# v loads on ACT's hardware queue, W_spatial and W_out requested at a later place, and the first q cast on VectorE

## The chip, the cores and the metric

The kernel runs on one core of one Trainium2 chip. The metric is the device time of one launch, in microseconds (us). A time is the median of all runs of a kernel; ratios and their intervals use runs in the fast state alone, and profiled runs are in the fast state unless the text says otherwise. Every kernel here gave a correct result. Times of different chips are not set against each other.

## The reference

Two layers follow one another. The first is a linear attention with decay, in blocks, over 4 batches, 8 heads, 768 tokens and 64 channels. The second is a gated MLP with a product over the tokens (W_spatial) in its middle.

```python
# attention: per block of 64 tokens, with a state carried from block to block
intra = einsum('bhic,bhjc->bhij', qb, kb) * Dmask
out   = einsum('bhij,bhjd->bhid', intra, vb) + einsum('bhid,bhde->bhie', qb * lam_pow, kv_state)
kv_state = lam_block * kv_state + einsum('bhsd,bhse->bhde', kb * rev_pow, vb)
# gated MLP on x = the attention's output, 4 x 768 x 512
h = maximum(x @ w_in, 0);  u, v = split(h)          # 512 columns each
v_n = normalise(v)
out = (u * (einsum('ts,bsd->btd', w_spatial, v_n) + b_spatial)) @ w_out
```

q, k and v are 6.3 MB each and are read once; W_spatial, its bias and W_out are read once for all batches.

## The kernel before

The kernel goes in 12 steps of 256 tokens (4 batches of 3). Each step loads k, q and v, all on SP's queue, in that order; casts them (k times a decay on VectorE or GpSimd, q on ACT, v on GpSimd); transposes k and q on TensorE; and computes scores, state and output. `xT` is the output of a step, brought by ACT from PSUM to SBUF in bf16; the products `pv` and `pu` with the two halves of W_in read it. The products with W_spatial and W_out of a batch are put between the attention steps of the next, and fill TensorE there.

Only TensorE and GpSimd keep the order of the text (`manual_schedule`). The order of instructions on ACT, VectorE and SP is chosen at compile time.

```python
    lam_bc = const.tile([P, H], FP32)
    nc.scalar.dma_start(out=lam_bc, in_=lam.unsqueeze(0).to_broadcast((P, H)))
    def load_step(n):
        # ... tiles q_in, k_in, v_in from a pool of 4 buffers each ...
        for c in range(2):
            nc.sync.dma_start(out=k_in[:, :, c, :], in_=...)      # 256 KB, rows of 256 bytes
        nc.sync.dma_start(out=q_in..., in_=...)                   # 512 KB, rows of 512 bytes
        for c in range(2):
            nc.sync.dma_start(out=v_in[:, :, c, :], in_=...)      # 256 KB, rows of 256 bytes
    load_step(0)
    krev = iota_f(...); qpos = iota_f(...); rel = iota_f(...)     # GpSimd iota, cast on VectorE
    load_win(DH, DFF)                                             # half of W_in, GpSimd's queue
    for n in range(1, 4):
        load_step(n)
    # ... ACT: loglam = Ln(lam_bc), ldec = Exp(loglam * krev), lq from qpos ...
    def cast_step(n):
        eng = nc.vector if n < NR else nc.gpsimd
        eng.tensor_tensor(out=kd..., in0=s["k_in"], in1=ldec..., op=ALU.mult)
        nc.scalar.activation(out=qc..., in_=s["q_in"], func=AF.Copy)
        nc.gpsimd.tensor_copy(out=vc, in_=s["v_in"])
    # trans_step: pt <- kd, qc (TensorE); kT <- pt (ACT); qT <- pt * lq (VectorE)
    # scores_step: pam <- qT, kT (TensorE); a <- pam * mask (VectorE)
    # kv_step: pkv <- vc, kd (TensorE).  out_step: pat <- qT, s, a, vc (TensorE); xT <- pat (ACT)
    with tc.manual_schedule(engines={PE, mybir.EngineType.Pool}):
        cast_step(0)
        load_win(0, DH)
        cast_step(1)
        nc.gpsimd.dma_start(out=wsp_raw, in_=...)                 # W_spatial, 1152 KB
        nc.gpsimd.dma_start(out=bsp_bc, in_=...)
        nc.gpsimd.dma_start(out=wout_sb, in_=...)                 # W_out, 512 KB
        trans_step(0); scores_step(0); kv_step(0); trans_step(1)
        load_step(4)
        for n in range(NS):
            if n + 2 < NS: cast_step(n + 2)
            if n + 5 < NS: load_step(n + 5)
            if n + 1 < NS: scores_step(n + 1)
            out_step(n)
            # ... queue pv, pu and the products with W_spatial and W_out ...
            if n + 1 < NS: kv_step(n + 1)
            fill(f // 2)
            if n + 2 < NS: trans_step(n + 2)
            fill(f - f // 2)
```

Of the kernel before, what the change touches and what calls it, by code (L numbers as in the profile page):

```python
# [9 lines left out]
FP32 = mybir.dt.float32  # L10
BF16 = mybir.dt.bfloat16
I32 = mybir.dt.int32
AF = mybir.ActivationFunctionType
# [5 lines left out]
def kernel(  # L19
# [12 lines left out]
    nc = tc.nc  # L32
    P = 128
    B, H, S, D = q.shape
# [6 lines left out]
    NR = S // (2 * P)  # L41
    NS = B * NR
    T2 = 2 * P
# [4 lines left out]
    fin = ctx.enter_context(tc.tile_pool(name="fin", bufs=4))  # L48
# [14 lines left out]
    st = {}  # L63

    def load_step(n):
        b, r = divmod(n, NR)
        toks = slice(r * T2, (r + 1) * T2)
        q_in = fin.tile([P, H, 2, D], FP32, tag="q_in", name=f"q_in_{n}")
        k_in = fin.tile([P, H, 2, D], FP32, tag="k_in", name=f"k_in_{n}")
        v_in = fin.tile([P, H, 2, D], FP32, tag="v_in", name=f"v_in_{n}")  # L70
        for c in range(2):
            nc.sync.dma_start(out=k_in[:, :, c, :],  # L72
                              in_=k[b, :, toks][:, c * P:(c + 1) * P].rearrange("h p d -> p h d"))
        nc.sync.dma_start(out=q_in.rearrange("p h m d -> p h (m d)"),  # L74
                          in_=q[b, :, toks].rearrange("h (p m) d -> p h (m d)", m=2))
        for c in range(2):
            nc.sync.dma_start(out=v_in[:, :, c, :],  # L77
                              in_=v[b, :, toks][:, c * P:(c + 1) * P].rearrange("h p d -> p h d"))
        st[n] = {"q_in": q_in, "k_in": k_in, "v_in": v_in}

    load_step(0)
    ident = const.tile([P, P], BF16)
    make_identity(nc, ident)

# [14 lines left out]
    wout_sb = wpool.tile([P, NCH, DM], BF16)  # L99
    bsp_bc = wpool.tile([P, S], BF16)  # L100
    wt_sb = wpool.tile([P, NBLK, S], BF16)
    wsp_raw = wpool.tile([P, NBLK, S], BF16)

    def load_win(f0, f1):
        nc.gpsimd.dma_start(out=win_sb[:, :, f0:f1],
                            in_=moe_w_in.rearrange("(g p) f -> p g f", p=P)[:, :, f0:f1])

    load_win(DH, DFF)
    for n in range(1, 4):
        load_step(n)  # L110
# [11 lines left out]
    for g in range(NG):  # L122
        nc.scalar.activation(out=lq[:, g, :], in_=qpos.rearrange("p m a d -> p (m a d)"),
                             func=AF.Exp, scale=logl[:, g:g + 1])
# [19 lines left out]
    def cast_step(n):  # L144
        s = st[n]
        kd = att.tile([P, 2, H, D], BF16, tag="kd", name=f"kd_{n}")
        qc = att.tile([P, 2, H, D], BF16, tag="qc", name=f"qc_{n}")
        vc = att.tile([P, H, 2, D], BF16, tag="vc", name=f"vc_{n}")
        eng = nc.vector if n < NR else nc.gpsimd
        eng.tensor_tensor(out=kd.rearrange("p c h d -> p h c d"), in0=s["k_in"],  # L150
                          in1=ldec.unsqueeze(2).unsqueeze(3).broadcast_to((P, H, 2, D)),
                          op=ALU.mult)
        nc.scalar.activation(out=qc.rearrange("p m h d -> p h m d"), in_=s["q_in"], func=AF.Copy)  # L153
        nc.gpsimd.tensor_copy(out=vc, in_=s["v_in"])  # L154
        s["kd"], s["qc"], s["vc"] = kd, qc, vc

    def trans_step(n):
        kd, qc = st[n]["kd"], st[n]["qc"]
        pt = two_banks([P, 2, NG, T2], f"pt_{n}", BF16)
        for j, src in ((0, kd), (1, qc)):  # L160
            for g in range(NG):
                for c in range(2):
                    nc.tensor.transpose(  # L163
                        out=pt[:, j, g, c * P:(c + 1) * P],
                        in_=src[:, c, 2 * g:2 * g + 2, :].rearrange("p h d -> p (h d)"),
                        identity=ident)
        kT = att.tile([P, NG, T2], BF16, tag="kT", name=f"kT_{n}")
        nc.scalar.activation(out=kT, in_=pt[:, 0], func=AF.Copy)  # L168
        qT = att.tile([P, NG, 2, 2, D], BF16, tag="qT", name=f"qT_{n}")
        nc.vector.tensor_tensor(out=qT.rearrange("p g m a d -> p g (m a d)"), in0=pt[:, 1],  # L170
                                in1=lq, op=ALU.mult)
        st[n]["qT"], st[n]["kT"] = qT, kT
# [4 lines left out]
    def scores_step(n):  # L177


        kT = st[n]["kT"]  # L180
        a_sb = att.tile([P, 2, 2, 2, 2, P], BF16, tag="a_sb", bufs=2, name=f"a_{n}")
        st[n]["a"] = a_sb
        for i in range(2):
            pam = two_banks([P, 2, 2, 2, P], f"pam_{n}_{i}")
            for g2 in range(2):
                for c in range(2):
                    for hh in range(2):
                        g = 2 * i + g2
                        nc.tensor.matmul(out=pam[:, hh, g2, c, :],  # L189
                                         lhsT=kT[hh * D:(hh + 1) * D, g, c * P:(c + 1) * P],  # L190
                                         rhs=qblk(n, g, hh, c), start=True, stop=True)
            nc.vector.tensor_tensor(  # L192
                out=a_sb[:, i].rearrange("p h g c x -> p (h g) c x"),
                in0=pam.rearrange("p h g c x -> p (h g) c x"),
                in1=amask[:, i].rearrange("p h g x -> p (h g) x").unsqueeze(2)
                .broadcast_to((P, 4, 2, P)), op=ALU.mult)
# [144 lines left out]
    def fill(n):  # L341
        for _ in range(min(n, len(pend))):
            pend.pop(0)()
# [12 lines left out]
            pend.extend([lambda i=i: po(b, i) for i in range(NR)])  # L356

    with tc.manual_schedule(engines={PE, mybir.EngineType.Pool}):
        cast_step(0)
        load_win(0, DH)  # L360
        cast_step(1)
        nc.gpsimd.dma_start(out=wsp_raw, in_=moe_w_spatial.rearrange("(a p) s -> p a s", p=P))
        nc.gpsimd.dma_start(out=bsp_bc, in_=moe_b_spatial.unsqueeze(0).to_broadcast((P, S)))
        nc.gpsimd.dma_start(out=wout_sb, in_=moe_w_out.rearrange("(t p) f -> p t f", p=P))
        trans_step(0)
        scores_step(0)
        kv_step(0)
        trans_step(1)
        load_step(4)
        fills = {0: 1, 1: 2, 2: 5}  # L370
        for n in range(NS):
            if n + 2 < NS:
                cast_step(n + 2)
            if n + 5 < NS:
                load_step(n + 5)
            if n + 1 < NS:
                scores_step(n + 1)
            out_step(n)
            after_out(n)
            if n + 1 < NS:  # L380
                kv_step(n + 1)
            f = fills.get(n, 4 + (n % 3 == 0))
            fill(f // 2)
            if n + 2 < NS:
                trans_step(n + 2)
            fill(f - f // 2)
        fill(len(pend))
# [30 lines left out]
```

## Time and profile before

| kernel before | |
|---|---|
| time, median of 3 runs (range) | 184.18 us (183.65 to 187.49) |
| time and span of the profiled run | 188.46 us, 186.7 us |
| TensorE busy | 145.7 us, 78% |
| ACT busy | 89.1 us, 48% |
| first instruction of TensorE | 14.3 us |

The profiled run took 4 us more than the median.

Three more views are needed for the comparison; the third stands behind the prediction. The first is the page's chain of work that ended last, as shares of the span (SPq and ACTq are issues of transfers):

```profile
PE 54%; SPq 13%; DVE 11%; ACT 9%; DMA 9%; issue 2%; POOL 1%; ACTq 0%; POOLq 0%
```

The second is the sum over one early stretch (start and end, length, then busy time and count of PE, PEld, DVE, ACT and POOL, granted clock, DMA share, GB/s). The third is the timeline: start, length, engine and line, operation, out<-in, and in brackets the idle time before it with what ended it. First VectorE's row, then ACT's two.

```profile
13.50:24.40 10.90, 6.39 (x83) 5.61 (x85) 10.04 (x20) 4.22 (x6) 2.17 (x2) 1.00 1.04 215
```

```profile
4.50 0.15 DVE L89 CAST krev<-krev_i 128x1 f32<-128x1 int32 x1
```

```profile
25.96 1.31 ACT L252 ACTIVATE xT<-pat 128x1024 bf16<-128x1024 f32 x1 [3.41 <-PE pat L249]
28.19 1.06 ACT L153 ACTIVATE qc<-q_in 128x1024 bf16<-128x1024 f32 x1 [0.92 <-DMA q_in<-in_q_dram]
```

The small cast `krev`, which the decay `ldec` needs, is done at 4.6 us. ACT brings the first `xT` at 25.96 us, **before** the next cast that has to wait for a q.

### The profile page before, as it was taken

The page shows a single profiled execution, that of the slowest core. Times are in us where ns is not written, and L with a number is a line of the kernel's source. Part 1 is how long each engine was busy: PE and PEld are TensorE (multiplying, and loading weights), DVE is VectorE, ACT ScalarE, POOL GpSimd, SP SyncE. Part 2 cuts the span into 40 slices and gives each one's busy share as a digit, 9 for nine tenths or more (in the row PEclk, how much of TensorE's full clock was granted, in tenths as well). Part 3 has the DMA queues.
Part 4 walks back from the last instruction along what each step waited for, and adds up shares of the span by engine and source line. Part 5 has one row for each costly group of instructions (what it writes and reads, how often), then busy time and mean ns, then how long its engine had stood idle before and what let it go on. Part 6 is the DMA issues. An engine that isn't in the chain of part 4 may idle for free.

```text
span 186.7 us, 3638 instructions
## 1 busy us (share of the span) xinstructions
PE 145.7 (78%) x1540; PEld 96.5 (52%) x1540; DVE 103.4 (55%) x191; ACT 89.1 (48%) x98; POOL 34.8 (19%) x35
## 2 busy tenths in 40 slices
PE   0005677507979779999997999999799999999980
PEld 0005563305649556655776665575676646565430
DVE  1029993705399853542989747169884722564400
ACT  4244324712677942268775613666722157660051
POOL 4004060006245344060606005020000000000000
PEclk9999996975999979999999999999999999999999
DMA  4999969999999999999998900530000027000035
GB/s 98 218 211 252 205 161 184 199 212 232 199 241 248 200 239 238 221 225 222 330 254 195 252 8 0 208 133 4 0 0 4 2 79 262 0 0 4 0 132 205
DMA packets 68337, 28.36 MB, mean 152 GB/s; under 512 B 50528, under 2 KB 65248, under 8 KB 68320
## 3 DMA queue, kind: packets, MB, share of 16 engines
q1 hardware_dynamic: 65664, 25.17, 56.5%
q0 software_dynamic: 2512, 2.95, 9.6%
q8 instruction: 12, 0.20, 0.5%
q14 instruction: 5, 0.04, 0.1%
q10 hardware_dynamic: 144, 0.00, 0.0%
HBM read 24.78 MB, written 6.29 MB: 166 GB/s over the span
## 4 chain that ended last, share of the span: by engine, by line
PE 54%; SPq 13%; DVE 11%; ACT 9%; DMA 9%; issue 2%; POOL 1%; ACTq 0%; POOLq 0%
PE pvs L307 17%; PE po L322 11%; DMA v_in<-in_v_dram 9%; PE pv L277 8%; PE pu L297 7%; SPq L77 6%; SPq L72 5%; PE pt L163 4%; DVE a L192 3%; PE pvs L309 3%; SPq L74 3%; DVE st L282 3%; ACT vh L280 2%; ACT wt_sb L336 2%; DVE vn L288 2%
## 5 line engine op out<-in xcount | busy, mean ns | idle before, releaser
L307 PE MATMUL pvs<-wt_sb,vn 128*128 128x384 bf16 x192 | 37.8, 331 | 2.1 <-ACT wt_sb L336 2.0
L192 DVE TENSOR_TENSOR a<-pam,amask 128x1024 bf16<-128x1024 f32 x24 | 28.5, 1210 | 6.0 <-PE pam L189 6.0
L154 POOL CAST vc<-v_in 128x1024 bf16<-128x1024 f32 x12 | 12.9, 1074 | 84.0 <-DMA v_in<-in_v_dram 42.7
L252 ACT ACTIVATE xT<-pat 128x1024 bf16<-128x1024 f32 x12 | 15.8, 1320 | 23.7 <-PE pat L249 23.6
L307 PEld LDWEIGHTS <-vn 128*128 128x128 bf16 x192 | 18.9, 99 | 14.9 <-issue 2.5
L297 PE MATMUL pu<-xT,win_sb 128*128 128x256 bf16 x192 | 24.4, 285 | 1.9 <-DVE a L192 1.9
L311 DVE TENSOR_TENSOR gT<-pvs,uT 128x768 bf16<-128x768 f32 x16 | 15.3, 958 | 18.2 <-PE pvs L309 18.1
L277 PE MATMUL pv<-win_sb,xT 128*128 128x512 bf16 x96 | 24.2, 400 | 1.2 <-ACT xT L252 1.2
L322 PE MATMUL po<-wout_sb,gT 128*128 128x512 bf16 x96 | 21.9, 379 | 1.5 <-DVE a L192 1.1
L297 PEld LDWEIGHTS <-win_sb 128*128 128x128 bf16 x192 | 19.2, 102 | 5.7 <-issue 1.8
L153 ACT ACTIVATE qc<-q_in 128x1024 bf16<-128x1024 f32 x12 | 12.7, 1055 | 19.0 <-DMA q_in<-in_q_dram 19.0
L325 ACT ACTIVATE o<-po 128x1024 f32<-128x1024 f32 x12 | 12.3, 1025 | 19.0 <-PE po L322 19.0
L282 DVE BATCH_NORM_STATS2 st<-vh 128x6 f32<-128x512 bf16 x24 | 15.6, 682 | 10.4 <-ACT vh L280 10.3
L163 PE MATMUL pt<-ident,kd 128*128 128x128 bf16 x96 | 8.6, 242 | 15.5 <-DVE kd L150 15.5
L170 DVE TENSOR_TENSOR qT<-pt,lq 128x1024 bf16<-128x1024 bf16 x12 | 8.2, 684 | 18.5 <-ACT kT L168 18.5
L150 POOL TENSOR_TENSOR kd<-k_in,ldec 128x1024 bf16<-128x1024 f32 x9 | 17.1, 1897 | 6.1 <-DMA k_in<-in_k_dram 6.1
L168 ACT ACTIVATE kT<-pt 128x1024 bf16<-128x1024 bf16 x12 | 12.2, 1021 | 11.2 <-PE pt L163 11.2
L280 ACT ACTIVATE vh<-pv 128x1024 bf16<-128x1024 f32 x12 | 12.3, 1024 | 8.8 <-PE pv L277 8.8
L163 PEld LDWEIGHTS <-kd 128*128 128x128 bf16 x96 | 7.2, 110 | 17.4 <-DVE kd L150 15.7
L277 PEld LDWEIGHTS <-xT 128*128 128x128 bf16 x96 | 9.5, 102 | 11.7 <-issue 1.7
L322 PEld LDWEIGHTS <-gT 128*128 128x128 bf16 x96 | 9.2, 98 | 11.9 <-issue 1.0
L299 ACT ACTIVATE uT<-pu 128x1024 bf16<-128x1024 f32 x12 | 12.2, 1020 | 5.9 <-PE pu L297 5.8
(52 smaller groups left out, 146.2 us busy)
## 6 DMA issues: line engine op xcount, KB each, us to landing
k_in<-in_k_dram SPq DMA_DIRECT2D x24, 256.0 KB, 5.8
q_in<-in_q_dram SPq DMA_DIRECT2D x12, 512.0 KB, 6.1
v_in<-in_v_dram SPq DMA_DIRECT2D x24, 256.0 KB, 6.0
out_dram<-o SPq DMA_DIRECT2D x12, 512.0 KB, 3.4
wsp_raw<-in_moe_w_spatial_dram POOLq DMA_DIRECT2D x1, 1152.0 KB, 11.3
win_sb<-in_moe_w_in_dram POOLq DMA_DIRECT2D x2, 512.0 KB, 8.4
wout_sb<-in_moe_w_out_dram POOLq DMA_DIRECT2D x1, 512.0 KB, 14.8
bsp_bc<-in_moe_b_spatial_dram POOLq DMA_DIRECT2D x1, 192.0 KB, 11.7
```

Of the source, the lines that this page charges most:

```text
L150: eng.tensor_tensor(out=kd.rearrange("p c h d -> p h c d"), in0=s["k_in"], in1=ldec.unsqueeze(2).unsqueeze(3).broadcast_to((P, H, 2, D)), ...
L154: nc.gpsimd.tensor_copy(out=vc, in_=s["v_in"])
L163: nc.tensor.transpose(out=pt[:, j, g, c * P:(c + 1) * P], in_=src[:, c, 2 * g:2 * g + 2, :].rearrange("p h d -> p (h d)"), identity=ident)
L192: nc.vector.tensor_tensor(out=a_sb[:, i].rearrange("p h g c x -> p (h g) c x"), in0=pam.rearrange("p h g c x -> p (h g) c x"), in1=amask[: ...
L252: nc.scalar.activation(out=xT[b][:, r].rearrange("p g (c d m) -> p (g c) m d", c=2, m=2), in_=po.rearrange("p g c (m d) -> p (g c) m d", m ...
L277: nc.tensor.matmul(out=ps[:, j], lhsT=x[:, r, c, j * P:(j + 1) * P], rhs=win_sb[:, c, DH:DFF], start=(c == 0), stop=(c == NCH - 1))
L280: nc.scalar.activation(out=vh[:, pair, :], in_=ps, func=AF.Relu)
L282: nc.vector.bn_stats(out=m["st6"][:, t, :], in_=vh[:, t, :])
L297: nc.tensor.matmul(out=ps[:, f], lhsT=win_sb[:, c, f * P:(f + 1) * P], rhs=x[:, r, c, :], start=(c == 0), stop=(c == NCH - 1))
L307: nc.tensor.matmul(out=ps[:, i, 0:HW_], lhsT=m["vn"][:, s, f * P:(f + 1) * P], rhs=wt_sb[:, s, cols], start=(s == 0), stop=False)
L311: nc.vector.tensor_tensor(out=m["gT"][:, f, :].rearrange("p (i x) -> p i x", i=2), in0=ps[:, :, 0:HW_], in1=m["uT"][:, f, :].rearrange("p ...
L322: nc.tensor.matmul(out=ps[:, j], lhsT=gT[:, c, t * P:(t + 1) * P], rhs=wout_sb[:, c, :], start=(c == 0), stop=(c == NCH - 1))
```

## The change

Its intent is to take the v loads off SP's blocked queue and give them a ring of their own, to move 1856 KB of weights away from the loads that TensorE waits for, and to free ACT of the first q cast.

```diff
 def load_step(n):
-    v_in = fin.tile(...)                       # k and q stay on SP
-    for c in range(2):
-        nc.sync.dma_start(out=v_in[:, :, c, :], in_=...)
+def load_v(n):
+    v_in = fin.tile(...)
+    for c in range(2):
+        nc.scalar.dma_start(out=v_in[:, :, c, :], in_=...)
 load_step(0)
+load_v(0)
 ...
-    nc.scalar.activation(out=qc..., in_=s["q_in"], func=AF.Copy)
+    if n == 0:
+        nc.vector.tensor_copy(out=qc..., in_=s["q_in"])
+    else:
+        nc.scalar.activation(out=qc..., in_=s["q_in"], func=AF.Copy)
 ...
+    load_v(1)
     cast_step(0)
     load_win(0, DH)
+    load_v(2)
     cast_step(1)
-    nc.gpsimd.dma_start(out=wsp_raw, ...); nc.gpsimd.dma_start(out=bsp_bc, ...)
-    nc.gpsimd.dma_start(out=wout_sb, ...)
 ...
     for n in range(NS):
         if n + 2 < NS: cast_step(n + 2)
+        if n + 3 < NS: load_v(n + 3)
+        if n == 0:
+            nc.gpsimd.dma_start(out=wsp_raw, ...); nc.gpsimd.dma_start(out=bsp_bc, ...)
+            nc.gpsimd.dma_start(out=wout_sb, ...)
```

More of the change, by code (lines that the diff above doesn't have):

```diff
@@ L69, in load_step @@
         k_in = fin.tile([P, H, 2, D], FP32, tag="k_in", name=f"k_in_{n}")
-        v_in = fin.tile([P, H, 2, D], FP32, tag="v_in", name=f"v_in_{n}")
         for c in range(2):
@@ L75, in load_step @@
                           in_=q[b, :, toks].rearrange("h (p m) d -> p h (m d)", m=2))
+        st[n] = {"q_in": q_in, "k_in": k_in}
+    def load_v(n):
+        b, r = divmod(n, NR)
+        toks = slice(r * T2, (r + 1) * T2)
+        v_in = fin.tile([P, H, 2, D], FP32, tag="v_in", name=f"v_in_{n}")
         for c in range(2):
-            nc.sync.dma_start(out=v_in[:, :, c, :],
+            nc.scalar.dma_start(out=v_in[:, :, c, :],
                               in_=v[b, :, toks][:, c * P:(c + 1) * P].rearrange("h p d -> p h d"))
-        st[n] = {"q_in": q_in, "k_in": k_in, "v_in": v_in}
+        st[n]["v_in"] = v_in
     load_step(0)
+    load_v(0)
     ident = const.tile([P, P], BF16)
@@ L152, in cast_step @@
                           op=ALU.mult)
-        nc.scalar.activation(out=qc.rearrange("p m h d -> p h m d"), in_=s["q_in"], func=AF.Copy)
+        qo = qc.rearrange("p m h d -> p h m d")
+        if n == 0:
+            nc.vector.tensor_copy(out=qo, in_=s["q_in"])
+        else:
+            nc.scalar.activation(out=qo, in_=s["q_in"], func=AF.Copy)
         nc.gpsimd.tensor_copy(out=vc, in_=s["v_in"])
@@ L358 @@
     with tc.manual_schedule(engines={PE, mybir.EngineType.Pool}):
+        load_v(1)
         cast_step(0)
         load_win(0, DH)
+        load_v(2)
         cast_step(1)
-        nc.gpsimd.dma_start(out=wsp_raw, in_=moe_w_spatial.rearrange("(a p) s -> p a s", p=P))
-        nc.gpsimd.dma_start(out=bsp_bc, in_=moe_b_spatial.unsqueeze(0).to_broadcast((P, S)))
-        nc.gpsimd.dma_start(out=wout_sb, in_=moe_w_out.rearrange("(t p) f -> p t f", p=P))
         trans_step(0)
@@ L373 @@
                 cast_step(n + 2)
+            if n + 3 < NS:
+                load_v(n + 3)
+            if n == 0:
+                nc.gpsimd.dma_start(out=wsp_raw,
+                                    in_=moe_w_spatial.rearrange("(a p) s -> p a s", p=P))
+                nc.gpsimd.dma_start(out=bsp_bc,
+                                    in_=moe_b_spatial.unsqueeze(0).to_broadcast((P, S)))
+                nc.gpsimd.dma_start(out=wout_sb,
+                                    in_=moe_w_out.rearrange("(t p) f -> p t f", p=P))
             if n + 5 < NS:
```

## The prediction

> **What bounds the kernel now.** I read the slices of the span first, then the sums by stretch, then the waits, then the chain that ended last, and last the queue's own issues. The slices of the kernel before (a digit is the busy share of one fortieth, 4.67 us, in tenths):
>
> ```profile
> PE   0005677507979779999997999999799999999980
> ...
> PEclk9999996975999979999999999999999999999999
> DMA  4999969999999999999998900530000027000035
> ```
>
> The reader is to see two regimes. From slice 9 on (about 43 us) TensorE is full to the end. Before it TensorE is half empty while the DMA row is at 9. The sums by stretch (length, then busy time and count of PE, PEld, DVE, ACT, POOL, then clock, DMA share, GB/s) say the same in numbers:
>
> ```profile
> 24.40:42.00 17.60, 8.28 (x112) 5.06 (x113) 9.09 (x14) 7.30 (x7) 3.12 (x5) 0.85 1.04 194
> 42.00:48.00 6.00, 4.91 (x42) 3.74 (x42) 2.58 (x4) 2.03 (x3) 2.93 (x2) 0.60 1.10 229
> ...
> 43.00:182.00 139.00, 131.00 (x1348) 85.85 (x1347) 82.83 (x151) 72.16 (x77) 26.29 (x19) 0.97 0.57 138
> 14.30:43.00 28.70, 14.68 (x192) 10.67 (x193) 18.32 (x32) 10.72 (x11) 5.70 (x7) 0.89 1.03 200
> ```
>
> After 43 us TensorE is busy 131.0 of 139.0 us, so no transfer can give much there. From its first instruction at 14.3 us to 43 us it idles 28.7 - 14.7 = 14.0 us. That, with the 14.3 us of start, is all that a change of loads can win. The longest piece of it is in the waits of the first 48 us (total, times, longest):
>
> ```profile
> POOL vc L154 <- DMA v_in<-in_v_dram: 33.9, 3, 14.4
> ...
> PE pkv L207 <- POOL vc L154: 8.1, 1, 8.1
> DVE kd L150 <- ACT ldec L120: 8.1, 1, 8.1
> ```
>
> and in the chain that ended last (start, length, what):
>
> ```profile
> 25.91 15.96 DMA v_in<-in_v_dram
> ...
> 42.00 1.05 POOL vc L154
> 43.09 0.43 PE pkv L207 x6
> ```
>
> So v of step 2 is asked for at 25.9 us and lands 16 us later, where a load of that line takes 6.0 us at the median; GpSimd casts it, and TensorE stands 8.1 us for it. What was beside it is in the issues of the three weights (KB, us to landing), asked for at 25.4 to 26.8 us:
>
> ```profile
> wsp_raw<-in_moe_w_spatial_dram POOLq DMA_DIRECT2D x1, 1152.0 KB, 11.3
> wout_sb<-in_moe_w_out_dram POOLq DMA_DIRECT2D x1, 512.0 KB, 14.8
> bsp_bc<-in_moe_b_spatial_dram POOLq DMA_DIRECT2D x1, 192.0 KB, 11.7
> ```
>
> The last of them lands at 26.8 + 14.8 = 41.6 us, just when v does. Their first reader is the transpose of W_spatial at 59.1 us, so they come 17 to 20 us early. SP meanwhile is blocked in issuing: its two k loads of step 3 take 10.0 us together from 26.5 us, its q load 5.2 us from 36.6 us.
>
> **What the Trainium skill says.** "DMA: Bandwidth & Descriptors", section "Issuing engines are not separate DMA queues": DMAs of all issuing engines run on the same 16 engines and interleave; another issuer only saves issue time. The DMA row, at 9 with a share of 1.03, agrees that the engines themselves are taken, so a second queue alone should add little. The same page, "Queues, rings and completion order": each DMA engine goes round-robin between its queue rows by packet. The trace agrees in kind: from 25.4 to 41.9 us (16.5 us) 198 GB/s in 11.3 us and 212 in 5.2 us make 3.34 MB; the weights are 1856 KB = 1.90 MB of it, so SP's ring got 1.44 MB, 87 GB/s, against 226 GB/s in the stretch 48 to 79 us, where it is alone. A second ring of loads should get a second turn, and its bytes come at the cost of k and q too. "Perfetto Trace Analysis", section "DMA Instruction — HWDGE (DVE, Sync)": the descriptor generator is shared and locked for one issuer at a time, and the recorded duration of an issue is lock wait plus generation. No run here shows an ACT issue under load (its one, of lam, took 0.42 us at the start), but the v issues on SP took 0.58 to 5.10 us, 1.31 at the median, so this is the price that ACT may have to pay, in order with its activations.
>
> **The change part by part.**
> First, weights later. The alone-cost of the weights: 16.5 us less what SP's 1.44 MB would need at 226 GB/s (6.4 us) gives 10.1 us. Taken from in front of v of step 2, it would land at 41.9 - 10.1 = 31.8 us, and 8 us of TensorE's idle time could go. The cold clock would go too: the 16 matmuls of pu after the stall took 3.54 us against 1.91 us later, 1.6 us. The ceiling of this part is so 8 + 1.6, some 9.7 us. But the weights don't vanish. The next loads in need are k and q of step 3: q landed at about 45.6 us (issued 36.6, 9.0 to landing), was cast at 45.7 to 46.8, and its transposes began at 46.8 to 47.3 us, with no slack at all. If 10 us of weights now lie between v of step 2 and q of step 3, the stall only moves by the 4 us of pkv and pu work that stands between. Counting bytes: k and q of steps 0 to 3 are 4.19 MB (18.6 us at 226 GB/s), v of 0 to 2 1.57 MB (7.0 us), the two halves of W_in about 6 us (an estimate from the weights' 10.1 us for 1.90 MB), and 2.5 us of start: 34 us without any weight, 44 us with all, against 45.6 before. With half of the weights ahead of q it is about 40 to 42 us. TensorE's dense part would then start 3 to 5 us earlier; I take 3.5 us as the likely gain here.
>
> Second, v on ACT's queue. 24 issues of 256 KB leave SP (24 x 1.3 = 31 us of its time) and go to ACT. On ACT unblocked ones cost 0.4 to 0.6 us, so 10 to 14 us; under load 1.3 us and a lock wait, so 31 us or more. ACT is busy 89.1 of 186.7 us, so it has room on average, but kT, xT and vh (1.0 to 1.3 us each) release TensorE. In the stage 44 to 80 us ACT is busy 20.7 of 36 us; two loads per step of 1.3 to 2.6 us fill a part of the rest. I charge 1 us of path for it, an estimate.
>
> Third, q of step 0 on VectorE instead of ACT: one cast of 128x1024, about 1.06 us on either. In the trace ACT computed ldec only after that cast (q landed 11.8, cast to 12.8, ldec 12.7), so kd of step 0 started at 13.1 though k had landed by 6. Now kd can be early, and TensorE may start 1 to 2 us sooner; as the loads bind next, this is worth 0 to 0.5 us.
>
> The sum: 3.5 - 1.0 + 0.3 = 2.8 us, so 184.2 - 2.8, about 181.4; I say 181.5.
>
> **The rivals.** (a) The requests are not later. They stand behind the cast of v of step 2 on GpSimd, so they leave when that v lands. ACT's v loads of steps 0 to 3 wait for nothing (four buffers), so they may all be issued at the start and take every other turn; v of step 2 would then land near 24 to 27 us, ahead of its own k and q, and the weights would leave at 25 us as before and now hold up q of step 2. TensorE would then stand at the transposes of step 2 until about 42 us, and pay more afterwards: 186 to 189 us. For it speaks that the weights' starting condition is v alone; against it, that k, q and v had one order before and somebody gave the loads this order by hand. (b) Two rings raise the rate. The share above 1 (1.18 in 48 to 60 us) shows that packets overlap; if 226 became 260 GB/s, the 34 us counted above would become some 30, and q of step 3 lands before 40 us: 175 to 178 us. Against it is the full DMA row. (c) ACT becomes the bound: issues that block it for 2 to 5 us at the start delay lam, ldec and the first kT, and later xT. Before, nothing of ACT waits for SP's blocked queue. This would make 184 to 188 us. (d) Hidden anyway: the stall moves from v of step 2 to q of step 3, everything else stays: 183 to 185 us.
>
> **Range and chances.** (b) and the plain working together give the side below 180.5 us, to about 175; (d) with a small gain gives the middle; (a) and (c) give up to 189. The plain working lies near the border of 2%, so I give faster 0.40, same 0.37, slower 0.23, and the range 175 to 189 us.
>
> **What would show it.** Right, if pkv of step 2 no longer waits 8 us for vc, the weights are requested at 28 to 33 us, and TensorE's full part begins 3 to 5 us earlier. The moved stall would be a wait of the transposes pt on qc or kd of step 3. Rival (a): weights requested before 27 us and pt of step 2 waiting for q. Rival (b): over 245 GB/s between 15 and 60 us. Rival (c): ACT issues of v over 2 us and a late loglam or kT. The prediction is wrong if the two rings share otherwise than by turns, or if ACT's order of issue is not the program's.

## The result, and the profile after

The changed kernel took **202.57 us** at the median of 4 runs (200.40 to 202.71); the kernel before, in 4 runs beside it, 184.54 us (183.65 to 187.49). The ratio is 1.097, with a 95% interval from 1.086 to 1.107. A ratio here is the mean time of one kernel's fast runs over that of the other's of the same rounds, so it is not quite the ratio of the two medians. The predicted range ended at 189 us. All outputs are right.

The slices of the span after (a fortieth is now 5.02 us; tenths of busy time):

```profile
PE   0001224907978758995999799999989999999980
...
PEclk9999999975999996998799999999999999999999
DMA  3999999999999999999820000052000006100034
```

TensorE starts later, does little in slices 3 to 6 (15 to 35 us) and nothing in slice 8, just past 40 us. The DMA row is at 9 from slice 1 to slice 18, about 95 us, and then falls away: the loads are done. The chain that ended last:

```profile
PE 40%; DMA 22%; SPq 14%; DVE 8%; ACT 7%; ACTq 4%; issue 2%; DVEq 0%
```

Transfers were 9% of the chain and are 22%; issues of transfers on ACT, which were 0%, are 4%. Three stretches of it, with the columns as before:

```profile
13.50:24.40 10.90, 1.89 (x16) 1.62 (x16) 6.03 (x15) 3.10 (x7) 1.17 (x1) 1.00 1.27 237
24.40:42.00 17.60, 8.12 (x120) 7.19 (x120) 11.93 (x15) 2.85 (x3) 5.01 (x5) 1.00 1.22 228
42.00:48.00 6.00, 1.76 (x5) 0.67 (x6) 0.69 (x1) 3.12 (x3) 1.11 (x2) 0.59 1.22 252
```

The loads came **faster**: 237, 228 and 252 GB/s where the kernel before had 215, 194 and 229. TensorE used less of it: 1.89 us busy instead of 6.39 in the first stretch. So the loss does not lie in the speed of the transfers as a whole. (Which load comes first is another matter: the cast of q of step 0 starts at 14.41 us, before at 11.77.) The same points of TensorE's work in both traces (start in us):

| point of TensorE's order | before | after | lag |
|---|---|---|---|
| transposes of step 0 | 14.33 | 19.50 | 5.2 |
| scores of step 0 | 18.05 | 28.78 | 10.7 |
| transposes of step 2 | 27.56 | 38.24 | 10.7 |
| product pv of step 0 | 29.76 | 46.24 | 16.5 |
| transposes of step 3 | 46.83 | 54.06 | 7.2 |
| transposes of W_spatial | 59.08 | 66.98 | 7.9 |
| first product with W_out | 79.82 | 89.46 | 9.6 |
| its last third | 84.17 | 97.97 | 13.8 |
| product with W_out, second batch | 114.58 | 128.35 | 13.8 |

The lag grows to 16.5 us, falls to 7.2 because the kernel before has its own stall of 8.1 us at 35 to 43 us, and takes its last jump, 4.2 us, at 90 to 98 us: 2.3 us of it are a wait, the rest are slower matmuls behind the wait (3.02 us for eight products with W_out, the eight before the wait 1.89). From there the two kernels run at the same pace. Three causes can be read off the timeline. The first two are in **VectorE's order** after the change:

```profile
14.41 0.69 DVE L161 CAST qc<-q_in 128x1024 bf16<-128x1024 f32 x1 [9.36 <-DMA q_in<-in_q_dram]
15.02 0.15 DVE L95 CAST krev<-krev_i 128x1 f32<-128x1 int32 x1
...
26.90 1.22 DVE L156 TENSOR_TENSOR kd<-k_in,ldec 128x1024 bf16<-128x1024 f32 x1 [6.32 <-DMA k_in<-in_k_dram]
28.04 0.68 DVE L180 TENSOR_TENSOR qT<-pt,lq 128x1024 bf16<-128x1024 bf16 x1
```

The moved cast of q was put in front of the casts of `krev` and its kin, and so `krev` waits for a q it has nothing to do with: 15.02 us instead of 4.50. `ldec` is then there at 15.5 us, but `kd` of step 0 starts only at 18.23: VectorE first builds the masks for `a` (15.54 to 18.3 us), which stood behind `kd` before. Later `kd` of step 2, which waits 6.3 us for its k, stands in front of `qT` of step 0, whose input is long there; the scores of step 0 wait for that `qT`. In **ACT's order**:

```profile
15.20 0.30 ACT L126 ACTIVATE ldec<-loglam,krev 128x8 f32<-128x8 f32 x1 [8.28 <-DVE krev L95]
...
43.93 1.06 ACT L163 ACTIVATE qc<-q_in 128x1024 bf16<-128x1024 f32 x1 [10.66 <-DMA q_in<-in_q_dram]
44.90 1.29 ACT L262 ACTIVATE xT<-pat 128x1024 bf16<-128x1024 f32 x1
...
81.98 10.30 ACTq L82 DMA_DIRECT2D v_in<-in_v_dram  x4
92.33 1.30 ACT L262 ACTIVATE xT<-pat 128x1024 bf16<-128x1024 f32 x1 [9.69 <-DMA v_in<-in_v_dram]
```

The cast of q of step 3 now stands ahead of the first `xT` and holds it for a load: 44.90 instead of 25.96 us. That brings the lag to 16.5 us at `pv`. And at 82 to 92 us ACT computes nothing for 9.7 us: four v issues stand ahead of `xT`, which could have run from 89.0 us, when its products were done. TensorE's rows for both:

```profile
46.24 3.60 PE L287 MATMUL pv<-win_sb,xT 128*128 128x512 bf16 x8 [6.27 <-ACT xT L262]
...
93.69 3.02 PE L332 MATMUL po<-wout_sb,gT 128*128 128x512 bf16 x8 [2.34 <-ACT xT L262]
```

What holds the v issues? The compiled program, listed by engine with the semaphores that each instruction waits for, has a part of the answer. Here are ACT's rows around that place in the changed kernel:

```
57 Activation qc_8  <- q_in_8            [waits Activation_49]
58 DMACopy    v_in_9  <- in_v_dram       [waits DMAHW7_49, Pool_49]
59 DMACopy    v_in_9  <- in_v_dram       [waits DMAHW0_49]
60 DMACopy    v_in_10 <- in_v_dram       [waits DMAHW5_49, DMAHW1_49, Pool_49]
61 DMACopy    v_in_10 <- in_v_dram       [waits DMAHW2_49]
62 Activation xT_1    <- pat_4           [waits PE_49]
```

All loads on hardware queues, SP's and ACT's together, share eight completion semaphores (DMAHW0 to DMAHW7) in turn. Each issue from the ninth on waits until an earlier transfer that had the same semaphore has landed. (A wait for Pool is one for the cast that frees the buffer; the last of these casts started at 72.08 us.) In the kernel before the same waits stand on SP, where nothing but transfers stands behind them. On ACT they stand in front of `xT`, `kT` and `vh`.

Not all of the 10.3 us is such a wait. The landings are in the trace, and can be matched to the issues by the semaphores of the compiled program. The four issues are recorded with 0.38, 0.78, 1.13 and 4.23 us; only between the first and the second lies a wait for a landing, of 3.6 us. The last and longest:

```profile
88.06 4.23 ACTq L82 DMA_DIRECT2D v_in<-in_v_dram  x1
```

The landing that it had to wait for came at 87.39 us, before it started. So what holds `xT` from 89.0 to 92.3 us is the length of an issue itself, and no run here shows what makes an issue so long. As for the order, the Trainium skill, "PSUM — Partial Sum Buffer", section "Engine vs sequencer instructions", calls ScalarE's queue strictly first in, first out; the trace agrees: `xT` at 92.33 starts 0.05 us after the last of the four issues.

The weights, last, were not later at all:

```profile
26.93 0.83 POOL L386 DMA_DIRECT2D wsp_raw<-in_moe_w_spatial_dram  x1
```

They were requested at 25.44 us before. They wait for the cast of v of step 2, and that v now lands earlier.

### The profile page after: what moved, and what is told of

Its sections match the earlier page's. It is cut to its first block, busy times and chain, and to the rows that moved or that the text cites. A ratio compares the mean times of both kernels' runs of the same rounds, so it can differ in the third digit from the quotient of the medians.

```text
span 200.9 us, 3637 instructions
## 1 busy us (share of the span) xinstructions
PE 146.4 (73%) x1540; PEld 97.2 (48%) x1540; DVE 102.9 (51%) x192; ACT 86.8 (43%) x97; POOL 34.6 (17%) x35
## 4 chain that ended last, share of the span: by engine, by line
PE 40%; DMA 22%; SPq 14%; DVE 8%; ACT 7%; ACTq 4%; issue 2%; DVEq 0%
DMA k_in<-in_k_dram 12%; PE pvs L317 11%; SPq L71 11%; DMA q_in<-in_q_dram 10%; PE po L332 10%; PE pv L287 7%; PE pu L307 5%; ACTq L82 4%; SPq L73 4%; DVE a L202 3%; PE pt L173 2%; ACT vh L290 2%; PE pvs L319 2%; DVE st L292 2%; ACT xT L262 1%
## 5 line engine op out<-in xcount | busy, mean ns | idle before, releaser
L317 PEld LDWEIGHTS <-vn 128*128 128x128 bf16 x192 | 18.8, 99 | 14.9 <-issue 2.9
L332 PE MATMUL po<-wout_sb,gT 128*128 128x512 bf16 x96 | 23.2, 393 | 3.9 <-ACT xT L262 2.3
L307 PE MATMUL pu<-xT,win_sb 128*128 128x256 bf16 x192 | 22.8, 273 | 2.5 <-DVE a L202 2.0
L173 PE MATMUL pt<-ident,kd 128*128 128x128 bf16 x96 | 9.5, 258 | 19.5 <-DVE kd L156 19.5
L163 ACT ACTIVATE qc<-q_in 128x1024 bf16<-128x1024 f32 x11 | 11.6, 1053 | 25.1 <-DMA q_in<-in_q_dram 25.1
L307 PEld LDWEIGHTS <-win_sb 128*128 128x128 bf16 x192 | 18.5, 98 | 5.6 <-issue 2.4
L173 PEld LDWEIGHTS <-kd 128*128 128x128 bf16 x96 | 7.9, 117 | 21.5 <-DVE kd L156 19.5
L156 POOL TENSOR_TENSOR kd<-k_in,ldec 128x1024 bf16<-128x1024 f32 x9 | 17.2, 1917 | 6.2 <-DVE qT L180 3.1
L199 PE MATMUL pam<-qT,kT 64*128 64x128 bf16 x192 | 8.3, 233 | 12.1 <-DVE qT L180 12.1
L178 ACT ACTIVATE kT<-pt 128x1024 bf16<-128x1024 bf16 x12 | 12.2, 1017 | 11.0 <-PE pt L173 7.3
L309 ACT ACTIVATE uT<-pu 128x1024 bf16<-128x1024 f32 x12 | 12.2, 1018 | 4.7 <-PE pu L307 4.6
```

The costliest lines, as they stand in the source:

```text
L156: eng.tensor_tensor(out=kd.rearrange("p c h d -> p h c d"), in0=s["k_in"], in1=ldec.unsqueeze(2).unsqueeze(3).broadcast_to((P, H, 2, D)), ...
L173: nc.tensor.transpose(out=pt[:, j, g, c * P:(c + 1) * P], in_=src[:, c, 2 * g:2 * g + 2, :].rearrange("p h d -> p (h d)"), identity=ident)
L307: nc.tensor.matmul(out=ps[:, f], lhsT=win_sb[:, c, f * P:(f + 1) * P], rhs=x[:, r, c, :], start=(c == 0), stop=(c == NCH - 1))
L317: nc.tensor.matmul(out=ps[:, i, 0:HW_], lhsT=m["vn"][:, s, f * P:(f + 1) * P], rhs=wt_sb[:, s, cols], start=(s == 0), stop=False)
L332: nc.tensor.matmul(out=ps[:, j], lhsT=gT[:, c, t * P:(t + 1) * P], rhs=wout_sb[:, c, :], start=(c == 0), stop=(c == NCH - 1))
```

## The experiments

The theory after the result: (T1) the issues of v on ACT, by waits for earlier landings or by their own length, hold ACT's other work; (T2) the order chosen at compile time for ACT and VectorE puts casts that wait for loads ahead of work that TensorE needs; both come from moving v. The rivals: the weights' new place, the cast of q of step 0, and the share of the two rings. All ratios are to the kernel before on the same chip.

### The cast of q of step 0 back on ACT

```diff
-        if n == 0:
-            nc.vector.tensor_copy(out=qo, in_=s["q_in"])
-        else:
-            nc.scalar.activation(out=qo, in_=s["q_in"], func=AF.Copy)
+        nc.scalar.activation(out=qo, in_=s["q_in"], func=AF.Copy)
```

> The changed kernel with one part undone: the cast of q of step 0 is back on ACT. If the late start (first transposes at 19.5 instead of 14.3 us) comes from that cast standing ahead of the small position casts in VectorE's order, the first transposes start at 14 to 16 us again; if that lag is carried to the end, the time falls by 3 to 5 us to about 198. Rival: the lag of the start is swallowed later, because ACT's waits at its v loads set the pace; then the start is earlier but the time stays 200 to 203 us.

It measured 200.84 us, ratio 1.071 (1.064 to 1.078). The profiled run was slow, so its order is read and its times are taken as rough. The ratio is 2.6 points below the 1.097 of the changed kernel, some 5 us, and the two intervals do not meet: so the expected gain of 3 to 5 us is there, and 200.84 us looks like no gain only because the kernel before is slower on this chip (187.22 against 184.54 us). The start was mended: `kd` was transposed at 10.5 us. Yet the scores of step 0 began at 28.46 us, as in the changed kernel. VectorE's order tells why: `kd` of step 2 still stands ahead of `qT` of step 0.

```profile
26.55 1.26 DVE L156 TENSOR_TENSOR kd<-k_in,ldec 128x1024 bf16<-128x1024 f32 x1 [7.64 <-DMA k_in<-in_k_dram]
27.73 0.68 DVE L177 TENSOR_TENSOR qT<-pt,lq 128x1024 bf16<-128x1024 bf16 x1
```

The next loss is on ACT:

```profile
29.58 9.00 ACTq L82 DMA_DIRECT2D v_in<-in_v_dram  x1
38.63 1.02 ACT L175 ACTIVATE kT<-pt 128x1024 bf16<-128x1024 bf16 x1 [9.24 <-issue]
```

This `kT` is that of step 1, whose products were done at 31.9 us. One v issue, recorded with 9.00 us and waiting for no landing, holds it for 6.7 us. So the cast of q accounts for about a quarter of the loss, not for most of it; where this trace gains the 5 us was not settled.

### v back on SP, all else as changed

```diff
-            nc.scalar.dma_start(out=v_in[:, :, c, :],
+            nc.sync.dma_start(out=v_in[:, :, c, :],
```

> The changed kernel with one part undone: v is loaded from SP's queue again, q of step 0 still on VectorE, the weights still requested after the cast of v of step 2. If v on ACT's queue is the cause of the loss, nearly all of the 18 us come back: 181 to 186 us, and the transposes of step 0 start near 14 us although the cast of q of step 0 still stands ahead on VectorE. If the cast on VectorE or the place of the weights is the cause, it stays above 195.

It measured 193.06 us, ratio 1.031 (1.026 to 1.037): better than the change, but a miss against 181 to 186. The edit was not as clean as I took it to be. The place of `load_v` in the text made SP load k and q of steps 1 to 3 before v of step 1, so `vc` of step 1 came at 32.2 us and `pkv` waited 7.4 us for it. The run shows that 6.5 of the 9.7 points of loss, some 12 us, go with v on ACT; it does not show the rest to be due to the weights.

### The kernel before with only v on ACT

```diff
-            nc.sync.dma_start(out=v_in[:, :, c, :],
+            nc.scalar.dma_start(out=v_in[:, :, c, :],
```

> The kernel before with one part done alone: v on ACT's queue. In the built program ACT has all eight v issues of steps 0 to 3 ahead of its first activation, the last six each behind the landing of an earlier transfer. If ACT's in-order waits are the cause, ACT's first activation (loglam, 3.9 us before) comes after 15 us, the first transposes after 20 us, and the time is 200 to 210 us, so at least as long as with the whole change. If contention between the two rings and the weights is the cause rather than ACT's waits, it is 186 to 192.

It measured 205.28 us, ratio 1.097 (1.091 to 1.103): this one word costs as much as the whole change. ACT's timeline:

```profile
1.21 18.12 ACTq L77 DMA_DIRECT2D v_in<-in_v_dram  x8
...
20.66 0.21 ACT L114 ACTIVATE loglam<-lam_bc 128x8 f32<-128x8 f32 x1
```

All eight issues of steps 0 to 3 went ahead of ACT's first computation. `loglam`, at 3.89 us before, comes at 20.66, TensorE's first transposes at 24.75, and the scores of step 0 at 39.83. Eight issues of 0.37 us, as the shortest in the changed kernel, would take some 3 us. But little of the rest is waiting for landings. By the compiled program the last five of the eight (not six, as I had expected) wait for one, and the trace shows less than 1 us between the issues; 17.2 of the 18.1 us are the recorded lengths of the issues themselves. The third waits for nothing and is recorded with 3.34 us. So ACT's standing at its issues is shown here, but not as the wait for landings that I had expected.

The compiled order differs too. As in the changed kernel, the masks stand ahead of `kd` of step 0, `kd` of step 2 ahead of `qT` of step 0, and the cast of q of step 3 ahead of the first `xT`. None of the three is in the runs with v on SP, the one above and the two below. So they come with v on ACT.

The handwritten places of `load_v` in the change were evidently there to avoid this, and they do at the start: `loglam` came at 4.46 us in the changed kernel.

### The kernel before with only the weights at the later place

```diff
         cast_step(1)
-        nc.gpsimd.dma_start(out=wsp_raw, ...); ...
 ...
                 cast_step(n + 2)
+            if n == 0:
+                nc.gpsimd.dma_start(out=wsp_raw, ...); ...
```

> The kernel before with one part done alone: the weights requested after the cast of v of step 2 instead of step 1. The prediction's own first step: the weights leave at 31 to 33 us, v of step 2 lands about 10 us sooner, and the time falls by some 3.5 us to 180 to 182. Rival: the stall only moves to q of step 3, and it is 183 to 185 us.

It measured 189.24 us, ratio 1.009 (1.002 to 1.016), within 2%. The sums by stretch:

```profile
24.40:42.00 17.60, 14.24 (x206) 10.43 (x207) 12.37 (x21) 10.95 (x11) 5.04 (x5) 1.00 1.12 211
42.00:48.00 6.00, 0.00 (x0) 0.00 (x0) 2.22 (x5) 0.00 (x0) 0.74 (x1) 0.71 1.00 181
```

The old stall was gone: TensorE was busy for 14.24 us of 17.6, before 8.28. Here the weights were later, at 30.87 us. But then TensorE stood for the whole of 42 to 48 us, until v of step 3 had landed (47.2 us), and again for 4.6 us at 53.6 us. ACT's timeline shows the second wait:

```profile
51.32 1.06 ACT L153 ACTIVATE qc<-q_in 128x1024 bf16<-128x1024 f32 x1 [10.37 <-DMA q_in<-in_q_dram]
52.28 1.28 ACT L252 ACTIVATE xT<-pat 128x1024 bf16<-128x1024 f32 x1
```

The order of T2 again, here without any load on ACT. The weights' bytes only move the stall from v of step 2 to v of step 3 and q of step 4. (This displaced cast, of q of step 4, comes with the weights and not with v.)

### The kernel before with only the q cast of step 0 on VectorE

```diff
-        nc.scalar.activation(out=qc..., in_=s["q_in"], func=AF.Copy)
+        if n == 0: nc.vector.tensor_copy(out=qo, in_=s["q_in"])
+        else:      nc.scalar.activation(out=qo, in_=s["q_in"], func=AF.Copy)
```

> The kernel before with one part done alone: the cast of q of step 0 on VectorE. In the built program it stands ahead of the three position casts, so ldec, which comes from one of them, still waits for q: the start stays at 14 to 14.5 us and the time within 1% of before. If the cast on VectorE by itself costs the 2% that the version with v back on SP showed, it is 190 us or more on that chip's scale (ratio 1.02).

It measured 188.32 us, ratio 1.016 (1.011 to 1.021). VectorE's order again has this cast ahead of `krev`, and the first transposes start at 14.58 us, almost as before (14.33), because here q of step 0 is there for the cast at 12.17 us, in the changed kernel at 14.41. The time misses the expected 1%. Where the 1.6% come from was not settled; the traces cannot tell, as the traced execution of the kernel before was as long (188.46 us). Alone, the cast gains nothing.

### The order held, v on ACT, and its control with v on SP

To separate T1 from T2, the order on ACT and VectorE was held to that of the kernel before, but for a few neighbours that changed places, with ordering edges: the q cast of step n+2 behind `xT` of step n, `kd` of steps 1 and 2 behind `qT` of step 0 and the mask product `a` of step 1. The weights stayed at the old place.

```diff
+        with tc.issue_after(last["qT", 0]):
+            cast_k(1)
+        with tc.issue_after(last["kT", 0]):
+            cast_q(1)
+            load_v(2)                      # left out in the control
 ...
+            with tc.issue_after(last["xT", n]):
+                if n + 2 < NS: cast_q(n + 2)
+                if n + 3 < NS: load_v(n + 3)   # left out in the control
```

With v on ACT:

> The kernel before with v on ACT's queue, as the run with that part alone, but with the order of computing on ACT and VectorE held to that of the kernel before by issue-order edges (the cast of q of step n behind xT of step n-2, the casts of k of steps 1 and 2 behind qT of 0 and the scores of 1, each v load behind the xT two to three steps earlier). Weights as before. If the loss comes from the compiled order, which puts casts that wait for loads ahead of ready work, most of it goes: ratio 0.98 to 1.03. If it comes from ACT standing at its own v issues for earlier transfers, or from contention of the rings, the ratio stays above 1.05.

The control, the same edges with v on SP:

> Control for the edges: the kernel before with the same order edges and v on SP's queue. The built order differs from before only from step 5 on, so the ratio should be 0.99 to 1.01. If it is off by more, the edges themselves change the time and the run with v on ACT must be read against this one.

The control measured 188.52 us, ratio 1.008 (0.997 to 1.020; two of its four runs were slow): the edges alone change little. With v on ACT it was 195.60 us, ratio 1.056 (1.049 to 1.063). So with the order held, v on ACT still costs 1.056 - 1.008, some 4.8% or 9 us. Up to the transposes of step 3 this kernel kept up with the one before; the q part of them was 1.6 us **earlier** (45.68 against 47.27 us). Then ACT stood:

```profile
60.61 2.83 ACTq L82 DMA_DIRECT2D v_in<-in_v_dram  x2
63.49 1.02 ACT L296 ACTIVATE vh<-pv 128x1024 bf16<-128x1024 f32 x1 [8.75 <-DMA k_in<-in_k_dram]
```

`vh` waits 8.75 us, and what ended the wait is the landing of a **k** load, with which `vh` has no data in common. In the compiled program the issue of v of step 5 stands ahead of `vh` and waits for semaphores DMAHW7 and DMAHW3. Here the standing is a wait for landings: the two issues are recorded with 0.38 and 0.45 us and start at 60.61 and 62.99 us, and the landings before them, at 60.51 and 62.97 us, are those of k of step 7, which SP had asked for only at 54.9 us. This is T1 without T2. TensorE waited 4.9 us for that `vh`, and its granted clock from 60 to 79 us was 0.73, in the control 1.00. At the transposes before the wait (56.90 against 54.91 us) TensorE was 2.0 us behind the control, at the first product with W_out (85.79 against 77.02 us) 8.8 us.

This pair also measures the second ring: v on ACT had 243 and 224 GB/s in the stretches 13.5 to 24.4 and 24.4 to 42 us, the control 221 and 208. From 48 to 79 us the two differed by less than 2%.

### The order held, v on GpSimd's queue

```diff
-            nc.scalar.dma_start(out=v_in[:, :, c, :],
+            nc.gpsimd.dma_start(out=v_in[:, :, c, :],
```

> The same order edges, v on GpSimd's software queue, so a second ring beside SP's but without any issue in ACT's order. If a second ring is worth something once nothing of ACT waits for it, the ratio is 0.95 to 0.99; if v then arrives too early at the cost of k and q, or the weights stand behind v, it is 1.00 to 1.05.

It measured 197.95 us, ratio 1.065 (1.058 to 1.073); the profiled run was slow, so its times are rough. v landed early (casts of steps 1 and 2 at 16.6 and 21.5 us), so the weights, behind the first of these, left at 17.6 us, and k of step 3 came only at 47 us; its `kd` on GpSimd waited 23.1 us for it. TensorE was busy for 2.00 us of the 17.6 from 24.4 to 42 us. No v issue stands in ACT's order here. This is the mechanism of the prediction's rival (a), though with the weights at their old place: where v runs ahead, the weights run ahead too, and k and q pay.

### The order held, only v of steps 0 to 2 on ACT

```diff
-            load_v(2)              # and load_v(n + 3): now on SP, in load_step
+        with tc.issue_after(last["v", 1]):
+            trans_step(0)          # its kT stands behind the issue of v of step 1
+        with tc.issue_after(last["v", 2]):
+            trans_step(1)
```

> The version with v on ACT's queue and the order held (ratio 1.056), with one thing more undone: only v of steps 0, 1 and 2 is issued on ACT, v of step 3 and later on SP. In the run before, ACT stood from 54.7 to 63.5 us at its issue of v of step 5, behind the landing of a k load, while a finished pv waited. If that standing is the rest of the loss, it is gone here: ratio 0.98 to 1.01, and no ACT wait for a k load. If the rest comes from the two rings sharing the first 45 us, or from the weights beside them, it stays: 1.03 to 1.06.

It measured 191.15 us, ratio 1.022 (1.014 to 1.030), and missed what I had expected. My own edges did it: to fix the places of the issues I had put `kT` behind them, and the issues waited.

```profile
22.36 1.02 ACT L186 ACTIVATE kT<-pt 128x1024 bf16<-128x1024 bf16 x1 [6.44 <-DMA k_in<-in_k_dram]
32.01 1.02 ACT L186 ACTIVATE kT<-pt 128x1024 bf16<-128x1024 bf16 x1 [7.68 <-DMA v_in<-in_v_dram]
```

The late standing at 63 us was gone, and the same standing was made at two early places: 6.4 and 7.7 us, for which TensorE's scores waited 6.6 and 6.2 us. It is T1 once more, put where I chose.

### The order held, v on SP, the weights in pieces

The sums suggest another way to move the weights: not to one later place but spread, each piece behind the cast of one further v.

```diff
-        nc.gpsimd.dma_start(out=wsp_raw, ...); ...; nc.gpsimd.dma_start(out=wout_sb, ...)
 ...
+            if n < 3:              # after the cast of v of step n + 2
+                cols = slice(n * 2 * P, (n + 1) * 2 * P)
+                nc.gpsimd.dma_start(out=wsp_raw[:, :, cols], in_=...[:, :, cols])
+            if n == 2: nc.gpsimd.dma_start(out=bsp_bc, ...)
+            if n == 3: nc.gpsimd.dma_start(out=wout_sb, ...)
```

> Towards a better version: v on SP, order held, W_spatial in three column pieces requested after the casts of v of steps 2, 3 and 4, the bias with the last, W_out after that of step 5. With the weights moved in one piece the stall went from v of step 2 to v of step 3. If spreading them keeps every load only 2 to 4 us late, TensorE is dense from about 34 us and the time falls by 3 to 6 us: ratio 0.965 to 0.985. If the sum of bytes before step 4 sets it anyway, the ratio is 0.99 to 1.01.

It measured **180.59 us** (178.70 to 180.86), ratio 0.963 (0.955 to 0.970): faster than both kernels. The stretch that the kernel before half lost, and the slices (4.42 us each):

```profile
24.40:42.00 17.60, 14.22 (x179) 9.70 (x176) 11.79 (x20) 10.40 (x11) 6.15 (x7) 1.00 1.06 226
```

```profile
PE   0004766968887899999979999999799999999980
```

TensorE was busy 14.22 us of 17.6, as with the weights at one later place, but here no stall followed: 4.84 us of the next 6 were busy. The compiled order of ACT and VectorE is the same as in the control above (ratio 1.008), so the gain comes from the weights' places. The requests left at 31.4, 40.8, 48.2 and 59.0 us.

### The same, with all v on ACT, and with only v of step 0 on ACT

```diff
-            nc.sync.dma_start(out=v_in[:, :, c, :],       # all v, issued by load_v as above
+            nc.scalar.dma_start(out=v_in[:, :, c, :],
```

> The better version (weights spread, order held, v on SP; ratio 0.963) with one thing changed: all of v on ACT's queue, its issues at the same places in ACT's order as in the run with the order held. If v on ACT costs through ACT standing at the issues whatever the weights do, the ratio to before is 1.00 to 1.03, 4 to 6% above the better version, with ACT waits for k, q or v loads before kT, vh or xT. If the loss of that run came from the weights' collision with v, the two queues cost nothing now: 0.96 to 0.98.

```diff
-            nc.sync.dma_start(
+            (nc.scalar if n == 0 else nc.sync).dma_start(
```

> The better version with only v of step 0 on ACT's queue: its two issues wait for nothing in the built program, so ACT never stands at a load. It leaves the pure effect of a second ring in the first 14 us. If two rings share the engines by turns, v of step 0 lands near 11 instead of 14 us, q of step 0 1 to 2 us later, the first transposes 1 us later, and the ratio is 0.96 to 0.975. If a second ring by itself costs more than that, it is above 0.98.

With all v on ACT: 194.09 us, ratio 1.045 (1.010 to 1.081, so unclear by its interval): 8 points above the better version, where 4 to 6 were expected. From the list of waits:

```profile
ACT vh L296 <- DMA k_in<-in_k_dram: 12.2, 1, 12.2
PE pwt L349 <- ACT vh L296: 8.3, 1, 8.3
```

One standing of 12.2 us behind two v issues, recorded with 0.37 us each, and TensorE waits 8.3 us of it. With only v of step 0 on ACT: 181.27 us, ratio 0.979 (0.966 to 0.993), just outside the expected 0.96 to 0.975. Its two issues wait for no landing, so nothing stands. The interval overlaps that of the version without it; v of step 0 was cast 2.7 us earlier (11.41 against 14.15 us) while q of step 0 came 0.8 us later (12.90 against 12.14 us), and the first transposes too. It is no gain that these runs can show.

## Why the prediction was wrong

**What held.** The weights' cost and the stall that they make were read rightly: taking them out of the stretch brings TensorE from 8.28 to 14.2 us busy in it, in two experiments. Rival (d), that the stall only moves, is what the weights' move alone did (1.009), but it moved to v of step 3 and q of step 4, not to q of step 3. The weights had more slack than the 17 to 20 us counted: W_spatial landed at 36.7 us, 22 us before its reader, and W_out, at 41.6 us, is first read at 79.8. Rival (a) was right in its timing: with v on another queue the weights were requested at 26.93 us in the changed kernel, and on GpSimd's queue at 17.6 us. Rival (b) was right in sign, though under its mark of 245 GB/s until 42 us.

**The step that failed** is the second part of the sum: "I charge 1 us of path for it, an estimate." Taken out of the changed kernel, v on ACT gave back 6.5 points, about 12 us; alone, with all its early issues in front, it cost 1.097, about 18 us; with the order held and placed by hand, 4.8 points, some 9 us. The term had the wrong content, not only the wrong size. I priced the issues by their recorded lengths (0.4 to 0.6 us unblocked, 1.3 under load) and compared that with ACT's free time. Three things were left out:

- The order of computing. With v on ACT the compiled program puts `kd` of step 2 ahead of `qT` of step 0 and the cast of q of step 3 ahead of the first `xT`. In the changed kernel the lag grows there from 5.2 to 10.7 and from 10.7 to 16.5 us.
- The waits in front of an issue. Rival (a) said that the v loads of steps 0 to 3 "wait for nothing (four buffers)"; in the compiled program five of these eight issues wait for an earlier landing. The Trainium skill, "Perfetto Trace Analysis", section "DMA Instruction — HWDGE (DVE, Sync)", draws the semaphore wait ahead of the recorded window. The run with the order held agrees: two issues recorded with 0.38 and 0.45 us keep ACT from computing for 8.75 us.
- The long issues. The median of 1.3 us hides single ones of 3.5 us (v alone on ACT) and 4.23 us (the changed kernel), and ACT computes nothing behind them.

I had seen SP blocked for 10.0 us over two k loads in the kernel before. It was of the third kind, not the second: the landings that the two issues had to wait for came at 18.0 and 18.8 us, the issues start at 26.5 and 32.3 us, and are recorded with 5.74 and 4.25 us. No other engine was issuing on a hardware queue then, so a lock held by another issuer does not explain them; the cause stays open.

With the order held, the standing at the issues alone made 1.056 against 1.008 of its control. The rest up to 1.097 goes with the order chosen at compile time and the places of the issues. I have no run that splits these two further, and the effects need not add.

**Rival (c)** named the right engine and the right victims, "lam, ldec and the first kT, and later xT", with 184 to 188 us. Its issues of 2 to 5 us were there, up to 4.23 us in the changed kernel. It was too mild because waits and a new order come on top of them. Of its victims, `loglam` was hardly late (4.46 us), `ldec` came at 15.2 us, but through VectorE's order, and `xT` at 44.9 us, through the new order, and at 92.3 us, through the long issue.

**The first part**, "I take 3.5 us as the likely gain here", failed by its own condition. In the changed kernel the weights left 1.5 us later than before, not the 3 to 8 us that the working needed; and where they did leave later, alone, the time rose by 0.9%.

**The third part**, "Now kd can be early", worth 0 to 0.5 us, had the wrong sign. `kd` of step 0 came at 18.23 us, before at 13.05. I had asked what ACT would no longer have to do, but not what VectorE would have to do later: its casts of `krev`, `qpos` and `rel` stood behind the moved cast, and the masks, built ahead of `kd`, added 2.7 us.

**What the prediction said would make it wrong** was "if ACT's order of issue is not the program's". That happened, on ACT and VectorE both, and it deserved more than a last clause: only TensorE and GpSimd have a fixed order in this kernel, so a change of loads can reorder the other engines.

## What to carry to other kernels

An issue of a transfer costs its engine its own time, which here ran from 0.37 to 4.23 us on ACT (once 9.00 us), and every wait that stands in front of it, completion semaphores that are reused included; two queues that share them wait for each other's loads. So loads that wait belong on an engine whose queue holds nothing that others need, and an engine with work on the critical path should issue only loads that wait for nothing. Before a load is moved, list in the compiled order what stands behind it, and after the change compare the order on each engine that is not fixed. In this kernel large early weights were better spread piecewise behind the loads of the steps (0.963) than moved in one block (1.009), which only moved the stall.

## What the Trainium skill lacked or had wrong

- "DMA: Bandwidth & Descriptors", section "Issuing engines are not separate DMA queues", says that issuing from several engines only saves the time of issuing, which is usually small. Here it cost time, in two ways. The compiled program gives hardware-queue loads of both engines eight completion semaphores in turn, and the issue waits in the engine's own queue for an earlier landing: with the order held, such standings on ACT took 6.4 to 12.2 us. And single issues, 0.37 us at the shortest, were recorded with up to 4.23 us on ACT (9.00 us in a profile) and 9.04 us on SP, without a landing to wait for. v on ACT alone made the kernel 9.7% slower.
- The same section gives a second issuer no more bandwidth. With the order alike and the weights requested at 22.9 and 24.0 us, v on ACT's queue instead of SP's had 243 against 221 GB/s from 13.5 to 24.4 us and 224 against 208 from 24.4 to 42 us, with rows of 256 and 512 bytes, and no clear difference after 48 us. It is not proof of a gain by the ring itself: the kernel with the weights later and all loads on SP also had 240 GB/s in the first of these stretches.
- "DMA: Bandwidth & Descriptors", section "Queues, rings and completion order", says that each DMA engine takes turns between queues by packet, but not what a queue of large rows does to one of small rows. In the kernel before, 1856 KB of weights on GpSimd's queue held SP's ring to 87 GB/s, worked out in the prediction, against 226 alone. Putting v on GpSimd's queue as well made `kd` of step 3 wait for its k until 47.4 us.
- No page that I read says that an engine's standing behind its own issues shows in a trace as a wait of the next computation for an unrelated transfer, as in `vh` released by a k load after 8.75 us.
